# A two-layer decode step: keys and values as the streamed operand of TensorE, in column groups of four kv heads, and late loading of the first feed-forward weights

## The chip, the cores and the metric

The kernel runs on one core of one Trainium2 chip. The metric is the device time of one execution in microseconds (us). Times are medians of a few executions, with lowest and highest in brackets. A ratio is the one on record for the fast runs of two kernels in the same rounds on the same chip; it is not quite the quotient of the medians quoted beside it (they differ by up to 0.6%). Its 95% interval follows in square brackets. The kernel before was run again beside every experiment: its medians lay between 367 and 372 us from chip to chip, so kernels of different rounds are compared by their ratios. A run is called slow when it is more than 1.5% above the fastest run of the same kernel, and fast otherwise. Medians and ranges are of all runs: two of the five of v_stat were slow, and one each of early_w, before_6buf, best_4k (the profiled one) and best_half_4k. Stage times come from one profiled execution per kernel.

## The reference, cut to what matters

One token for each of four batch rows, 32 query heads, 8 kv heads, 4096 cached positions, head width 128, all bf16. The same attention and the same feed-forward are applied twice, with the same weights and caches, so each row needs its keys and its values twice. The kernels keep the transposed keys (K^T) of a row in memory between the layers and read K once; V is read twice.

```python
def _A_ref(x, k_cache, v_cache, wq, wo):
    q = ...                                       # x @ wq, 32 heads of 128
    k = jnp.repeat(k_cache, rep, axis=1)          # rep = 4 query heads a kv head
    v = jnp.repeat(v_cache, rep, axis=1)
    scores = jnp.einsum("bhqd,bhkd->bhqk", q, k) * (Dh ** -0.5)
    p = _softmax(scores, axis=-1)
    o = jnp.einsum("bhqk,bhkd->bhqd", p, v)
    return ... @ wo

x = x + _A_ref(_layernorm(x), A_k_cache, A_v_cache, A_wq, A_wo)
x = x + _B_ref(_layernorm(x), B_w_gate, B_w_up, B_w_down)
x = x + _A_ref(...)        # layer 2: the same caches and weights
x = x + _B_ref(...)
```

## The kernel before

The kernel works row by row: layer 1 of row b+1 shares a stretch of time with layer 2 of row b. In that stretch ("K/V stretch" below) a row's K arrives in chunks of 512 KB, DVE turns each into K^T, layer-2 scores of row b use the old K^T and layer-1 scores of row b+1 the new one, and V chunks of row b+1 follow. Then comes the "feed-forward stretch": output projection, feed-forward and query projection of row b+1, with the layer-2 V chunks of row b filling the gaps. DMA is issued in program order, into one ring of buffers.

In both attention products the cache is the *stationary* operand: a 128x128 block is loaded into the array and a few columns stream past it, 16 query columns for the scores, 4 probability columns for the values.

```python
KV_BUFS = 7                    # ring of 512 KB chunks of K and V
GH = 2                         # kv heads of one softmax round

def load_kv(cache, b, kvh, t, name):
    tl = kvin.tile([P, CH, Dh], BF16, name=name, tag="kv")
    src = cache[b, kvh].rearrange("(p c) d -> p c d", p=P)      # 4 KB a partition
    dq.dma_start(out=tl[:], in_=src[:, t * CH:(t + 1) * CH])
    return tl

def scores_head(sc, s, kt, kvh, qb):
    ...
    for g in range(G8):
        for be in range(BE):                  # 32 matmuls a head
            nc.tensor.matmul(sc[:, s, g, :], lhsT=kt[:, g, be // 2, :, be % 2],
                             rhs=qb[:, kvh, be].rearrange("p a h -> p (a h)"),
                             start=(be == 0), stop=(be == BE - 1))

def soft_exp(sc, gmax):
    ...                                       # DVE subtracts the maximum
    nc.scalar.activation(out=raw..., in_=sc..., func=ACT.Exp, scale=scale)   # contiguous

class Values: ...
    v = load_kv(A_v_cache, self.b, kvh, t, "v_t")
    for i in range(CH):                       # 16 matmuls a chunk
        c = t * CH + i
        nc.tensor.matmul(o, lhsT=v[:, i, :], rhs=pe[:, s, c, :],
                         start=(c == 0), stop=(c == C - 1))

def rest_weights(i): ...       # wq, wo, w_gate, w_up, w_down, one piece after each
                               # softmax round of the first attention
```

## Time and profile before

Median 372.08 us (371.13 to 372.81, 3 runs); the profiled span is 373.3 us. Stages are cut at the first score matmul of each row's K/V stretch and at the last layer-1 V chunk of that stretch, both read from the timeline.

| stage | us | sum |
|---|---|---|
| start, to the first scores of the first K/V stretch | 99.0 | 99.0 |
| three K/V stretches | 54.9, 49.7, 52.5 | 157.1 |
| three feed-forward stretches | 22.2, 27.6, 24.3 | 74.1 |
| tail: last layer-2 attention and feed-forward | 43.2 | 43.2 |

The page of the kernel before: first the busy time of the engines (us, share of the span, instructions), then GB/s in 40 slices, the chain of waits, and three groups (busy us, mean ns of one | idle before, what ended it).

```profile
PE 204.4 (55%) x6848; PEld 193.2 (52%) x6848; DVE 160.4 (43%) x502; ACT 26.5 (7%) x70; POOL 25.1 (7%) x70
...
GB/s 237 421 417 383 416 375 417 395 407 228 11 253 302 234 376 363 382 313 359 288 244 386 347 329 377 358 341 275 271 332 308 265 382 413 345 311 147 248 119 2
...
PE 38%; DMA 29%; issue 16%; DVE 15%; POOL 1%; ACT 1%; SPq 0%; ACTq 0%; POOLq 0%; DVEq 0%
...
L334 PE MATMUL ot<-pe,v_t 128*128 128x4 bf16 x2048 | 68.7, 167 | 77.2 <-DMA v_t<-in_A_v_cache_dram 60.1
...
L254 DVE STREAM_TRANSPOSE kt<-k_t 128x512 f32<-128x512 f32 x128 | 82.8, 686 | 26.9 <-DMA k_t<-in_A_k_cache_dram 16.8
...
L285 ACT ACTIVATE raw<-sc 128x256 bf16<-128x256 f32 x32 | 12.3, 383 | 222.6 <-DVE sc L281 222.6
```

No engine is full, and TensorE waits 60.1 us for V. DMA reaches 421 GB/s where nothing holds it up and falls to 11 GB/s at the first feed-forward (slice 11) and to 234 to 300 in the score phases. The kernel is a stream of cache bytes with holes in it.

What a chunk costs TensorE is seen in the timeline of the kernel before (start us, us, engine, line, operation, count):

```profile
270.64 1.85 PE L266 MATMUL sc<-qb,kt 128*128 128x16 bf16 x64
...
318.28 0.99 PE L334 MATMUL ot<-pe,v_t 128*128 128x4 bf16 x32
...
321.26 0.57 PE L334 MATMUL ot<-pe,v_t 128*128 128x4 bf16 x16
321.69 0.99 PE L166 MATMUL qps<-xn_bf,wq_sb 128*128 128x1 bf16 x32
...
370.00 0.59 PE L523 MATMUL xo_ps<-ident_bf,xoT 128*4 128x128 bf16 x4 [0.47 <-DVE xoT L520]
```

The 16 value matmuls of a chunk begin at 321.26 and the next group at 321.69: 0.43 us a chunk, about 27 ns for a weight load with its matmul. The Trainium skill ("TensorE: Matmul & The Clock Gate", Part 2, "Weight-path perf modes") says that weights of 128 bf16 columns take a fast load path; 27 ns for 128x128 cells agrees with it.

### The profile page before, as it was taken

To read this page: it belongs to the slowest core of one execution; us is meant where nothing else is said; L and a number is where in the kernel's file an instruction comes from. 1 tells how busy PE (TensorE), PEld (TensorE's weight loads), DVE (VectorE), ACT (ScalarE), POOL (GpSimd) and SP (SyncE) were. 2 spreads that over 40 slices of the span, in tenths; PEclk is the share of its full clock that TensorE was granted. 3 is DMA by queue.
4 is the path that set the end of the run, shared out by engine and by line. 5 is a ranking of instruction groups with operands and counts; after the bars stand their busy time and mean duration, and the time that the engine had idled before them with its cause. 6 is when DMAs were issued, how large, how long until landed. Compare 5 with 4: busy or idle time off the path is not lost.

```text
span 373.3 us, 14915 instructions
## 1 busy us (share of the span) xinstructions
PE 204.4 (55%) x6848; PEld 193.2 (52%) x6848; DVE 160.4 (43%) x502; ACT 26.5 (7%) x70; POOL 25.1 (7%) x70
## 2 busy tenths in 40 slices
PE   0435141337765545865555657656465557678645
PEld 0334141337665445764555647655465456677635
DVE  0854423303686553321777453127745523224104
ACT  0020000000011011000011010000101000001100
POOL 0000000000010111000111110000110100002000
DMA  7999999995078799999879899998888799984730
GB/s 237 421 417 383 416 375 417 395 407 228 11 253 302 234 376 363 382 313 359 288 244 386 347 329 377 358 341 275 271 332 308 265 382 413 345 311 147 248 119 2
DMA packets 36302, 115.52 MB, mean 309 GB/s; under 512 B 3208, under 2 KB 9104, under 8 KB 36240
## 3 DMA queue, kind: packets, MB, share of 16 engines
q1 hardware_dynamic: 36240, 114.58, 83.7%
q8 instruction: 53, 0.87, 0.9%
q14 instruction: 9, 0.07, 0.0%
HBM read 114.56 MB, written 0.00 MB: 307 GB/s over the span
## 4 chain that ended last, share of the span: by engine, by line
PE 38%; DMA 29%; issue 16%; DVE 15%; POOL 1%; ACT 1%; SPq 0%; ACTq 0%; POOLq 0%; DVEq 0%
DMA v_t<-in_A_v_cache_dram 29%; PE sc L266 11%; PE ot L334 10%; DVE kt L254 7%; PE qps L166 3%; PE y L190 3%; DVE colmax L273 2%; PE y L232 2%; PE hg L204 2%; PE hu L204 2%; PE x L293 1%; PE st L128 1%; DVE sc L281 1%; POOL gmax L275 1%; PE yf L190 1%
## 5 line engine op out<-in xcount | busy, mean ns | idle before, releaser
L334 PE MATMUL ot<-pe,v_t 128*128 128x4 bf16 x2048 | 68.7, 167 | 77.2 <-DMA v_t<-in_A_v_cache_dram 60.1
L334 PEld LDWEIGHTS <-v_t 128*128 128x128 bf16 x2048 | 63.7, 105 | 82.4 <-DMA v_t<-in_A_v_cache_dram 63.8
L254 DVE STREAM_TRANSPOSE kt<-k_t 128x512 f32<-128x512 f32 x128 | 82.8, 686 | 26.9 <-DMA k_t<-in_A_k_cache_dram 16.8
L266 PE MATMUL sc<-qb,kt 128*128 128x16 bf16 x2048 | 63.0, 175 | 17.5 <-issue 13.6
L266 PEld LDWEIGHTS <-kt 128*128 128x128 bf16 x2048 | 58.9, 104 | 20.0 <-issue 15.2
L273 DVE TENSOR_REDUCE colmax<-sc 128x8 f32<-128x256 f32 x32 | 13.4, 420 | 45.0 <-PE sc L266 45.0
L293 PE MATMUL x<-raw,ident_bf 128*32 128x64 bf16 x512 | 13.4, 238 | 31.1 <-ACT raw L285 28.6
L285 ACT ACTIVATE raw<-sc 128x256 bf16<-128x256 f32 x32 | 12.3, 383 | 222.6 <-DVE sc L281 222.6
L275 POOL PARTITION_ALL_REDUCE gmax<-colmax x32 | 11.9, 371 | 229.9 <-DVE colmax L273 149.7
L166 PE MATMUL qps<-xn_bf,wq_sb 128*128 128x1 bf16 (+1 forms) x640 | 20.2, 166 | 11.3 <-issue 10.1
L293 PEld LDWEIGHTS <-ident_bf 128*32 128x32 bf16 x512 | 9.8, 118 | 31.6 <-issue 30.9
L190 PEld LDWEIGHTS <-wo_sb 128*128 128x128 bf16 x640 | 19.8, 104 | 12.2 <-issue 12.2
L166 PEld LDWEIGHTS <-wq_sb 128*128 128x128 bf16 x640 | 18.9, 104 | 11.8 <-issue 11.2
L190 PE MATMUL y<-OT_bf,wo_sb 128*128 128x1 bf16 x512 | 15.8, 165 | 9.9 <-DVE OT_bf L338 6.7
L307 POOL PARTITION_ALL_REDUCE den<-cs x32 | 12.7, 398 | 85.7 <-DVE cs L304 85.7
L338 DVE TENSOR_TENSOR OT_bf<-ot,rden 128x8 bf16<-128x8 f32 (+1 forms) x23 | 3.5, 153 | 33.7 <-PE ot L334 33.7
L281 DVE TENSOR_TENSOR sc<-sc,gmax 128x256 f32<-128x256 f32 x32 | 13.5, 422 | 8.9 <-POOL gmax L275 8.7
L298 ACT CAST pe<-x 128x256 bf16<-128x256 f32 x32 | 11.9, 372 | 33.0 <-PE x L293 33.0
L304 DVE TENSOR_REDUCE cs<-raw 128x8 f32<-128x256 bf16 x32 | 12.4, 389 | 3.8 <-ACT raw L285 3.8
L171 DVE TENSOR_TENSOR q_bf<-qps,rstd 128x8 bf16<-128x8 f32 (+1 forms) x20 | 3.3, 170 | 24.0 <-PE qps L166 23.6
L197 DVE TENSOR_TENSOR XX<-XX,y 128x4 f32<-128x4 f32 (+1 forms) x9 | 1.4, 160 | 22.5 <-PE y L232 16.0
L179 DVE TENSOR_TENSOR qb<-qe,amask 128x128 bf16<-128x128 f32 (+1 forms) x23 | 7.8, 338 | 5.6 <-PE qe L177 5.5
(50 smaller groups left out, 113.2 us busy)
## 6 DMA issues: line engine op xcount, KB each, us to landing
v_t<-in_A_v_cache_dram SPq DMA_DIRECT2D x128, 512.0 KB, 7.4
k_t<-in_A_k_cache_dram SPq DMA_DIRECT2D x64, 512.0 KB, 8.8
wo_sb<-in_A_wo_dram SPq DMA_DIRECT2D x2, 2048.0 KB, 12.5
wq_sb<-in_A_wq_dram SPq DMA_DIRECT2D x2, 1024.0 KB, 9.2
wq_sb<-in_A_wq_dram SPq DMA_DIRECT2D x1, 2048.0 KB
wg_sb<-in_B_w_gate_dram SPq DMA_DIRECT2D x1, 1792.0 KB, 17.1
wu_sb<-in_B_w_up_dram SPq DMA_DIRECT2D x1, 1792.0 KB, 13.1
wd_sb<-in_B_w_down_dram SPq DMA_DIRECT2D x1, 1792.0 KB, 17.1
```

Source lines behind the costliest of these rows:

```text
L166: nc.tensor.matmul(qps[:, i, :], lhsT=wq_sb[:, k, m * Dh:(m + 1) * Dh], rhs=xn_bf[:, k, bs], start=(k == 0), stop=(k == KD - 1))
L190: nc.tensor.matmul(y[:, :, dk], lhsT=wo_sb[:, i, dk * P:(dk + 1) * P], rhs=rhs, start=(first and i == h0 and dk == 0), stop=(last and i == ...
L204: nc.tensor.matmul(h[:, m, :], lhsT=w_sb[:, k, m * P:(m + 1) * P], rhs=xn_bf[:, k, bs], start=(k == 0), stop=(k == KD - 1))
L254: nc.vector.transpose(out=self.kt[:, t * gt:(t + 1) * gt, bb].rearrange("p g c j -> p g (c j)"), in_=kf[:, :, bb])
L266: nc.tensor.matmul(sc[:, s, g, :], lhsT=kt[:, g, be // 2, :, be % 2], rhs=qb[:, kvh, be].rearrange("p a h -> p (a h)"), start=(be == 0), s ...
L273: nc.vector.tensor_reduce(out=colmax[:], in_=v, axis=AX.X, op=ALU.max)
L275: nc.gpsimd.partition_all_reduce(gmax.rearrange("p s h -> p (s h)"), colmax.rearrange("p s h -> p (s h)"), P, RED.max)
L281: nc.vector.tensor_tensor(out=w, in0=w, in1=gmax[:].unsqueeze(2).broadcast_to([P, GH, G8 * QD, rep]), op=ALU.subtract)
L293: nc.tensor.matmul(x[a * QS:(a + 1) * QS, :, :, cc, :], lhsT=ident_bf[:, cc * QS:(cc + 1) * QS], rhs=raw[:, :, :, a, :], start=True, stop= ...
L304: nc.vector.tensor_reduce(out=cs[:], in_=raw.rearrange("p s g a h -> p s h (g a)"), axis=AX.X, op=ALU.add)
L307: nc.gpsimd.partition_all_reduce(den.rearrange("p s h -> p (s h)"), cs.rearrange("p s h -> p (s h)"), P, RED.add)
L334: nc.tensor.matmul(o, lhsT=v[:, i, :], rhs=pe[:, s, c, :], start=(c == 0), stop=(c == C - 1))
```

## The change

The intent is to make the *cache* the streamed operand and the narrow queries and probabilities the stationary one, with the array split into four groups of 32 columns that work side by side. Four kv heads share one softmax round; a maximum over 512 columns and an exp with the maximum as bias replace DVE's subtraction and sum. The rest follows from it: V is read in rows of 2 KB (so that a chunk fits the new column order), exp writes its result permuted, the two halves of a value result are put together with masks (`sel_y`), and with the new tiles in memory only six of seven chunk buffers fit. Besides that, wo, w_gate, w_up and w_down are loaded behind the last V chunk of row 0 instead of during the first attention. The diff, cut to its core (renames, constants and the final recombination left out):

```diff
-GH = 2
-KV_BUFS = 7
+GH = 4
+KV_BUFS = 6
...
-def scores_head(sc, s, kt, kvh, qb):
-    for g in range(G8):
-        for be in range(BE):
-            nc.tensor.matmul(sc[:, s, g, :], lhsT=kt[...], rhs=qb[:, kvh, be]..., ...)
+def scores(kts, qb):                 # 32 matmuls for four heads
+    for s in range(2):
+        for be in range(BE):
+            for G in range(2):
+                for n in range(2):
+                    r0 = 32 * (2 * n + G)            # column group
+                    nc.tensor.matmul(sc[r0:r0 + 32, :],
+                        lhsT=qb[:, s, G * BE + be].rearrange("p a h -> p (a h)"),
+                        rhs=kt[:, be // 2, n * SN:(n + 1) * SN, be % 2],   # 512 columns
+                        ...)
...
+    nc.scalar.activation(out=p.rearrange("p g j c -> p g c j"),       # every 4th bf16
+                         in_=sc.rearrange("p (g c j) -> p g c j", g=HN, c=QD),
+                         func=ACT.Exp, bias=nm[:, 0:1], scale=scale, accum_out=ls[:])
...
+    src = A_v_cache[self.b, kvh].rearrange("(a q g) d -> q a g d", a=QD, g=KG)
-    for i in range(CH):
-        nc.tensor.matmul(o, lhsT=v[:, i, :], rhs=pe[:, s, c, :], ...)
+    for gl in range(HN):                 # 8 matmuls a chunk, on two column groups
+        for n in range(2):
+            r0 = 32 * (2 * n + G)
+            c0 = r0 + 16 * s + 8 * t
+            nc.tensor.matmul(self.acc[r0:r0 + 8, s], lhsT=pT[:, gl, c0:c0 + 8],
+                             rhs=v[:, :, n * HN + gl, :], ...)            # 256 columns
...
 # attend(), order of a row
+    sc2 = [scores(old K^T of four heads) for both groups]   # layer 2 of the row before
+    ... 8 K chunks turned, with the two softmax rounds between them ...
+    sc1 = scores([KT[i] for i in range(GH)], qb1[0])        # after all 8
...
+    if b1 == 0:      # after the last V of row 0
+        dq.dma_start(out=wo_sb..., ...); ... wg_sb, wu_sb, wd_sb
```

## The prediction

> **What bounds the kernel now.** Mostly the stream of keys, values and weights, broken by chains of compute. The page shows 114.58 MB loaded; in undisturbed stretches (the table of 10-us windows, 10 to 30 us) DMA moves about 418 GB/s, so the bytes alone need about 274 us of the 373.3. The rest is DMA idle or slow: nothing moves from 90 to 102 us (first feed-forward), 200 to 300 GB/s in the score phases of each batch row (100 to 130, 180 to 200, 250 to 270 us), about 10 us at the last feed-forward. No engine is full: PE 55%, DVE 43%. In the chain of waits the V load is only 29%, PE 38%, and "issue" 16%: pieces of 1.3 to 3.9 us in which PE waits for nothing but its instructions (the instruction queue moved 0.87 MB, as much as 2 x 6848 PE instructions of 64 B).
>
> **What the change removes.** 2048 score matmuls (a head, 32 of them plus loads, takes 0.86 us), 2048 value matmuls (0.43 us per 512 KB chunk) and 512 swap matmuls. It adds 512 matmuls of 512 columns, 1024 of 256 and 64 transposes; PE falls from 6848 to about 3900 matmuls. On DVE the score maximum, subtraction and sum (13.4 + 13.5 + 12.4 us) become 16 maxima of 512 columns and small operations, plus 32 accumulator reads: about 20 us less. POOL loses about 18 us. The 128 transposes of K (82.8 us busy, about 1.22 us a chunk in pairs) stay.
>
> **What decides it: do column groups run side by side?** This trace says yes: the 16 swap matmuls (four column groups, 64 columns) start within 0.17 us, and their cast follows 0.46 us after the first start. The Trainium skill ("TensorE: Matmul & The Clock Gate", Part 3) gives 2.38x for three column tiles at 512 columns, and 216 ns for one such matmul alone; 32 of them in four groups are then, as an estimate, 2.0 to 2.8 us for four heads, against 3.45 now. A value chunk alternates between two groups: about 0.45 us, as now. If they ran one after another, a score group would be 7 us and a chunk 0.85, and the kernel slower, about 400 us.
>
> **On the critical path.** (1) First feed-forward: its weights (10 MB, 24 us) now load behind the last V of row 0, under output projection, gate and up. The first scores of the next phase start near 90 us instead of 99. (2) A row's cycle is now 78.7, 75.7 and 77.1 us from its first score to the next row's (in the chain). I reckon about 68 to 72: fewer softmax rounds (2 groups, not 4), eight K chunks turned almost without interruption, scores 1.4 times as quick, fewer instruction stalls. DMA alone needs 60. (3) After the last K: 42.7 us now, about 37 then. Sum: 90 + 3 x 70 + 37 = 337.
>
> **What would show it.** Score matmuls of a quarter starting within tens of ns, a group of 32 in under 3 us; issue in the chain down to about 10%; DMA gap at the first feed-forward under 6 us; row cycle near 70 us; K transposes still 0.61 to 0.69 us each; mean rate about 340 GB/s.
>
> **What would make it wrong.** Column groups that serialize, through weight loads (the skill's "TensorEngine Tiling (Array Packing)", Restrictions, says column tiling disables fast weight load) or moving reads of every second bf16; V rows of 2 KB instead of 4 KB per descriptor slowing the stream; six buffers instead of seven running dry while softmax of four heads is awaited; instruction stalls that stay.
>
> Predicted 338 us, 318 to 364; faster 0.86, same 0.07, slower 0.07.

(In it, a row's cycle is quoted as 78.7, 75.7 and 77.1 us. Cut at the first score matmuls, as in the tables here, the three cycles of the kernel before are 77.1, 77.3 and 76.8. The 216 ns for a matmul of 512 columns stand in Part 2 of that page, not in Part 3, and hold at full clock.)

## The result, and the profile after

The kernel after takes 412.05 us (409.67 to 413.51, 4 runs) against 371.61 (369.93 to 372.81, 4 runs): ratio 1.1135 [1.1048, 1.1221]. It is slower by 11%, and outside the predicted range.

| stage | before | after | predicted |
|---|---|---|---|
| start | 99.0 | 102.7 | 90 |
| three K/V stretches | 157.1 | 168.7 | |
| three feed-forward stretches | 74.1 | 91.1 | |
| both, three rows | 231.2 | 259.8 | 3 x 70 = 210 |
| tail | 43.2 | 46.9 | 37 |
| profiled span | 373.3 | 409.4 | 337 |

Every stage is longer. The page of the kernel after, in the order in which before was shown, with the row of granted clock that before's page doesn't have:

```profile
PE 246.3 (60%) x3908; PEld 157.3 (38%) x3908; DVE 165.8 (40%) x513; ACT 34.0 (8%) x54; POOL 6.9 (2%) x22
...
PEclk9996565555656565655665656558555656556655
...
GB/s 273 312 348 384 367 268 334 378 375 277 82 294 210 382 270 336 367 347 183 270 237 338 355 239 366 322 307 170 276 215 387 241 333 362 331 193 61 359 95 2
...
L368 PE MATMUL acc<-v_t,pT 128*8 128x256 bf16 x1024 | 97.3, 397 | 42.2 <-DMA v_t<-in_A_v_cache_dram 39.4
L288 DVE STREAM_TRANSPOSE kt<-k_t 128x512 f32<-128x512 f32 x128 | 80.9, 683 | 35.8 <-DMA k_t<-in_A_k_cache_dram 35.8
...
L302 PE MATMUL sc<-kt,qb 128*32 128x512 bf16 x512 | 52.9, 590 | 16.5 <-DVE qb L210 16.5
L327 ACT ACTIVATE p<-sc,nm 128x512 bf16<-128x512 f32 x16 | 22.3, 1395 | 219.6 <-DVE junk L322 218.8
```

There are 43% fewer TensorE instructions, and TensorE is busy 42 us longer. The value products rose from 68.7 to 97.3 us. One exp takes 1395 ns for 512 columns, where before 256 took 383. The transposes of K are what they were. (The chain of waits of this profile could only be followed back over the last 38 us, so it isn't set beside the one of before.)

**The clock.** The row PEclk says that TensorE mostly ran near half clock. Its first three slices say 9, and before's page has no such row and says clock 1.000. Both are the absence of a record, not full speed. (In the windows of later sections, the 0.99 of best is so for the first 5 of its 12 us, and every 1.00 of best_half is so: their first records come at 99.6 and 322.3 us.) The timeline of the kernel after shows it; the first four lines are the first score group of the kernel (and the stationary loads that begin each four of its matmuls), the next two are the same four transposes of 128 columns at two times, then the same value chunk at two times:

```profile
25.73 3.60 PE L302 MATMUL sc<-kt,qb 128*32 128x512 bf16 x32 [0.52 <-DVE qb L210]
26.14 0.16 PEld L302 LDWEIGHTS <-qb 128*32 128x32 bf16 x4 [0.27 <-issue]
26.57 0.16 PEld L302 LDWEIGHTS <-qb 128*32 128x32 bf16 x4 [0.27 <-issue]
26.99 0.16 PEld L302 LDWEIGHTS <-qb 128*32 128x32 bf16 x4 [0.27 <-issue]
...
111.32 0.40 PE L335 MATMUL pt<-ident_bf,p 128*128 128x128 bf16 x4 [2.17 <-ACT p L327]
...
115.22 0.61 PE L335 MATMUL pt<-ident_bf,p 128*128 128x128 bf16 x4 [3.51 <-ACT p L327]
...
167.99 0.60 PE L368 MATMUL acc<-v_t,pT 128*8 128x256 bf16 x8
...
178.02 1.02 PE L368 MATMUL acc<-v_t,pT 128*8 128x256 bf16 x8
```

The windows around four of these, and the two stretches that follow the first score group, of the same kernel (window: length, busy us and count of PE, PEld, DVE, ACT, POOL, then granted clock, DMA share, GB/s):

```profile
111.30:111.75 0.45, 0.40 (x4) 0.23 (x4) 0.45 (x2) 0.00 (x0) 0.00 (x0) 1.00 0.69 255
115.20:115.85 0.65, 0.63 (x8) 0.61 (x8) 0.65 (x2) 0.00 (x0) 0.00 (x0) 0.50 0.75 265
...
178.00:179.05 1.05, 1.05 (x15) 0.45 (x13) 0.48 (x3) 0.00 (x0) 0.00 (x0) 0.50 1.04 402
25.70:29.40 3.70, 3.60 (x32) 1.08 (x32) 0.32 (x2) 0.00 (x0) 0.00 (x0) 1.00 1.03 420
29.90:33.20 3.30, 0.00 (x0) 0.00 (x0) 1.80 (x7) 1.48 (x2) 0.40 (x1) 1.00 1.03 395
33.40:57.10 23.70, 14.05 (x168) 6.97 (x168) 11.10 (x22) 1.59 (x3) 0.39 (x1) 0.50 0.96 351
```

Four transposes of 128 columns take 0.40 us where 1.00 was granted and 0.61 where 0.50 was. Four matmuls of 128 columns at the end of the kernel before took 0.59: half clock, under a heading of 1.000. The score group at 25.73 runs under "1.00" as well, and it starts four matmuls of 512 columns every 0.42 to 0.43 us. The Trainium skill ("TensorE: Matmul & The Clock Gate", Part 1) gives 426.7 ns as the distance of matmuls of 512 columns with the clock throttled to one half, its default, and 215.7 at full clock: this agrees with the first figure. The kernel after runs mostly at half clock (0.603 on its page, where the first 30 us without a record count as 1), the kernel before wherever its trace lets it be seen; and before the first record a profile shows 1. The first record of the kernel after is a grant of full clock at 29.85 us, half a microsecond after its first score group has ended, and 3.41 us later the clock is back at half: TensorE had nothing to do in between. Where two score groups follow each other, full clock comes in the middle of them, so their 64 matmuls take 6.48 us at 102.66 and not twice 3.60.

The prediction's own evidence agrees with half clock too: 16 swap matmuls of 64 columns on four column groups, started within 0.17 us, are four rounds about 53 ns apart, 0.83 ns a column.

This also answers what the prediction called decisive. Four transposes of 128 columns, 512 columns one after another, take 0.61 us with the latency of the last one; four matmuls of 512 columns on four column groups start every 0.43 us. The column groups do run side by side.

**The hole at the row's start.** The last part of the result is in the windows of 12 us from the first scores of the first K/V stretch, before and then after:

```profile
99.00:111.00 12.00, 7.35 (x259) 6.97 (x258) 9.80 (x22) 1.51 (x4) 1.53 (x4) 1.00 0.59 183
```

```profile
102.70:114.70 12.00, 6.84 (x70) 2.40 (x68) 8.73 (x21) 2.92 (x4) 0.77 (x2) 0.64 0.34 112
```

DMA moves 183 GB/s there in the kernel before and 112 in the kernel after. The timeline of the kernel after says why, in order of time:

```profile
102.66 6.48 PE L302 MATMUL sc<-kt,qb 128*32 128x512 bf16 x64
...
106.32 0.69 DVE L311 TENSOR_REDUCE m<-sc 128x1 f32<-128x512 f32 x1 [2.79 <-PE sc L302]
...
107.19 2.49 DVE L288 STREAM_TRANSPOSE kt<-k_t 128x512 f32<-128x512 f32 x4
...
108.52 5.44 SPq L284 DMA_DIRECT2D k_t<-in_A_k_cache_dram  x4
...
124.99 1.40 ACT L327 ACTIVATE p<-sc,nm 128x512 bf16<-128x512 f32 x1 [8.54 <-DVE junk L322]
```

Chunks of K lie ready in the ring, but their first transpose stands behind the row maximum in DVE's program, the maximum waits 2.79 us for the scores of a whole group of four heads, and only the transposes free chunk buffers. The next K loads are issued from 108.52 on. The last line is the exp of a later round; it matters below.

### The profile page after: what moved, and what is told of

It reads as the page before. It is cut to its first block, busy times and chain, and to the rows that moved or that the text cites. A ratio compares the mean times of both kernels' runs of the same rounds, so it can differ in the third digit from the quotient of the medians.

```text
span 409.4 us, 8903 instructions
## 1 busy us (share of the span) xinstructions
PE 246.3 (60%) x3908; PEld 157.3 (38%) x3908; DVE 165.8 (40%) x513; ACT 34.0 (8%) x54; POOL 6.9 (2%) x22
## 5 line engine op out<-in xcount | busy, mean ns | idle before, releaser
L368 PE MATMUL acc<-v_t,pT 128*8 128x256 bf16 x1024 | 97.3, 397 | 42.2 <-DMA v_t<-in_A_v_cache_dram 39.4
L368 PEld LDWEIGHTS <-pT 128*8 128x8 bf16 x1024 | 47.0, 111 | 74.8 <-issue 50.4
L302 PE MATMUL sc<-kt,qb 128*32 128x512 bf16 x512 | 52.9, 590 | 16.5 <-DVE qb L210 16.5
L327 ACT ACTIVATE p<-sc,nm 128x512 bf16<-128x512 f32 x16 | 22.3, 1395 | 219.6 <-DVE junk L322 218.8
L302 PEld LDWEIGHTS <-qb 128*32 128x32 bf16 x512 | 17.2, 134 | 44.7 <-issue 25.7
L311 DVE TENSOR_REDUCE m<-sc 128x1 f32<-128x512 f32 x16 | 11.0, 690 | 38.1 <-PE sc L302 38.1
L222 PE MATMUL y<-OT_bf,wo_sb 128*128 128x1 bf16 x512 | 14.9, 165 | 11.9 <-DMA wo_sb<-in_A_wo_dram 10.2
L388 PE MATMUL fin<-sel_o,o 128*128 128x8 f32 x64 | 15.4, 351 | 5.5 <-DVE o L376 5.5
L388 PEld LDWEIGHTS fin<-sel_o,o 128*128 128x128 f32 x64 | 14.2, 308 | 6.6 <-DVE o L376 6.6
L210 DVE TENSOR_TENSOR qb<-qe,sel 128x256 bf16<-128x256 f32 x32 | 11.8, 410 | 4.0 <-PE qe L205 4.0
L264 PE MATMUL y<-H_bf,wd_sb 128*128 128x1 bf16 (+1 forms) x280 | 8.6, 166 | 5.7 <-DMA wd_sb<-in_B_w_down_dram 3.7
```

The costliest lines, as they stand in the source:

```text
L210: nc.vector.tensor_tensor(out=qb[:, s], in0=qv[:, s].unsqueeze(2).broadcast_to([P, 2 * BE, 2 * QD, rep]), in1=sel2[:, s].unsqueeze(1).unsq ...
L222: nc.tensor.matmul(y[:, :, dk], lhsT=wo_sb[:, i, dk * P:(dk + 1) * P], rhs=rhs, start=(first and i == h0 and dk == 0), stop=(last and i == ...
L264: nc.tensor.matmul(y[:, :, dk], lhsT=wd_sb[:, k, dk * P:(dk + 1) * P], rhs=H_bf[:, k, :], start=(k == 0), stop=(k == KF - 1))
L302: nc.tensor.matmul(sc[r0:r0 + 32, :], lhsT=qb[:, s, G * BE + be].rearrange("p a h -> p (a h)"), rhs=kt[:, be // 2, n * SN:(n + 1) * SN, be ...
L311: nc.vector.tensor_reduce(out=m[:], in_=sc[:], axis=AX.X, op=ALU.max)
L327: nc.scalar.activation(out=p.rearrange("p g j c -> p g c j"), in_=sc.rearrange("p (g c j) -> p g c j", g=HN, c=QD), func=ACT.Exp, bias=nm[ ...
```

## The experiments

In these, "points" are per cent of the time of the kernel before in the same rounds; one point is 3.7 us. Of the seven runs of before beside v_stat7, half_sc7, exp_read and split7, three were slow.

| kernel | us (lowest to highest, runs) | ratio [95%] |
|---|---|---|
| after | 412.05 (409.67 to 413.51, 4) | 1.1135 [1.1048, 1.1221] |
| v_stat | 399.5 (393.72 to 400.39, 5) | 1.0813 [1.0725, 1.09] |
| v_four | 398.59 (398.24 to 400.98, 4) | 1.079 [1.0711, 1.0869] |
| v_wide | 411.88 (407.6 to 412.97, 4) | 1.1114 [1.1018, 1.121] |
| early_w | 421.89 (417.02 to 426.14, 4) | 1.1362 [1.1244, 1.148] |
| half_sc (wrong) | 378.85 (375.93 to 381.31, 4) | 1.0305 [1.021, 1.04] |
| exp_flat | 456.55 (455.39 to 461.25, 4) | 1.2446 [1.2331, 1.2561] |
| before_2k (wrong) | 362.76 (361.25 to 363.15, 4) | 0.9863 [0.979, 0.9936] |
| before_6buf | 389.4 (388.07 to 394.22, 4) | 1.0575 [1.0454, 1.0695] |
| v_stat7 | 389.45 (386.97 to 390.44, 4) | 1.0592 [1.0476, 1.0709] |
| half_sc7 (wrong) | 371.49 (369.4 to 372.52, 4) | 1.0106 [0.9997, 1.0215] |
| exp_read | 399.14 (397.01 to 400.54, 4) | 1.0865 [1.0711, 1.1019] |
| split7 | 371.01 (370.33 to 372.02, 4) | 1.0103 [1.0003, 1.0202] |
| best | 363.4 (362.73 to 363.92, 6) | 0.9793 [0.9739, 0.9847] |
| best_half (wrong) | 359.49 (357.12 to 360.11, 4) | 0.9674 [0.961, 0.9739] |
| best_half_4k (wrong) | 355.34 (353.39 to 358.89, 4) | 0.9623 [0.9539, 0.9708] |
| best_4k (wrong) | 362.73 (359.05 to 364.65, 4) | 0.9808 [0.9721, 0.9895] |
| best_four | 368.96 (367.75 to 371.22, 6) | 1.0014 [0.9963, 1.0065] |

The first theory (C in the texts below) was the clock: streamed columns cost twice what was reckoned. The rival (S) was the stream: DMA and DVE stand still at the start of a row because of order and buffers. Both turned out to hold parts, and neither the whole. The totals of v_stat, half_sc, v_stat7 and best_half_4k fell between the ranges that were expected, those of early_w, exp_flat, before_2k and before_6buf outside all of them, and that of exp_read 1 us under its range.

### Values stationary again (v_stat)

Only the value products go back to the form of before; scores, softmax, order and loads stay.

```diff
-                        nc.tensor.matmul(self.acc[r0:r0 + 8, s], lhsT=pT[:, gl, c0:c0 + 8],
-                                         rhs=v[:, :, n * HN + gl, :], ...)
+                            nc.tensor.matmul(self.acc[:, hl, :], lhsT=v[:, y, n * HN + gl, :],
+                                             rhs=pT[:, gl, c0:c0 + rep], ...)
```

> The changed kernel with one part undone: V is again the stationary operand (16 matmuls of 4 columns a chunk), all else as changed. Theory C (TensorE runs at half clock nearly everywhere, a streamed column costs 0.83 ns, so a value chunk costs 1.02 us instead of 0.43 us and the feed-forward stretches become TensorE-bound): chunk back to about 0.43 us, each of the three feed-forward stretches with values falls from about 30 us to 22 to 24 us, total 378 to 390 us. Theory S (the loss is the softmax chain of four heads, in which the six buffers run dry): total stays above 404 us, feed-forward stretches shorter but DMA idles as much after.

Measured: 399.5 us, 3.2 points less than after. The three feed-forward stretches fell from 91.1 to 81.3 us and the three K/V stretches stayed at 168.3. A feed-forward stretch in windows, after and then v_stat:

```profile
158.00:188.00 30.00, 27.79 (x522) 20.94 (x526) 10.65 (x51) 0.21 (x1) 0.00 (x0) 0.56 0.99 342
```

```profile
158.30:186.00 27.70, 19.67 (x642) 19.33 (x641) 7.58 (x45) 0.21 (x1) 0.00 (x0) 0.50 0.95 341
```

In the kernel after TensorE is busy 27.8 of 30 us there: it is the limit of that stretch. With stationary values it is busy 19.7. Of the 14.2 us between the two profiled spans, 9.8 come off the feed-forward stretches, 1.5 off the start and 2.5 off the tail; in the K/V stretch values were not the limit. The time came out between what the two theories expected, so neither covers it.

### Values on all four column groups (v_four) and on wider groups (v_wide)

In the change each value matmul takes 8 probability columns and half of the rows it makes are thrown away, on two of four groups. v_four splits each into two of 128 columns, one a group, with nothing thrown away. v_wide makes each matmul 32 columns wide, to see whether a busier array raises the clock; its extra rows are wrong.

```diff
 # v_four
+                        for y in range(HALF):
+                            r0 = 32 * (2 * n + y)
+                            nc.tensor.matmul(self.acc[r0:r0 + rep, hl, :],
+                                             lhsT=pT[:, gl, c0:c0 + rep],
+                                             rhs=v[:, y, n * HN + gl, :], ...)    # 128 columns
 # v_wide
-                        nc.tensor.matmul(self.acc[r0:r0 + 8, s], lhsT=pT[:, gl, c0:c0 + 8],
+                        nc.tensor.matmul(self.acc[r0:r0 + 32, s], lhsT=pT[:, gl, r0:r0 + 32],
```

> Values still stream, but as 16 matmuls of 128 columns on four column groups instead of 8 of 256 on two (no wasted rows), result gathered in bf16. Theory C: only the streamed columns per group and the clock count, so a chunk takes 4 x 107 = 0.43 us plus latency, and the total is that of the stationary form within 1.5%. If instead column groups or 4-column weight loads cost something of their own, a chunk stays at 0.6 us or more. Theory S: above 404 us.

> Wrong result on purpose: the values' stationary operand is 32 columns wide instead of 8, all else as changed. It streams the same columns but works four times as many cells. If the throttle grants clock by work done in the array and not by time busy, the granted clock rises clearly above 0.62 (0.75 or more), chunks fall towards 0.55 us and the total to 385 to 400 us. If it counts only busy time, clock 0.60 to 0.63 and 408 to 416 us.

Measured: v_four 398.59 us, the same as v_stat, so half of the streamed columns were waste and taking them away gains as much as the old form does. v_wide 411.88 us, the same as after, at a granted clock of 0.615 against 0.603: four times the cells at work does not raise the clock. (v_wide still passed the comparison with the reference although rows were wrong. The reference says why: run on a CPU with V set to zero, its output changes by 0.02 rms, beside an output of 2.5 rms. So the comparison can hardly see the attention, and a pass doesn't prove that a kernel is right.)

### Weights early again (early_w)

```diff
+    def rest_weights(i):     # wo, wo, w_gate, w_up, w_down, one a step of the first attention
...
-            dq.dma_start(out=wo_sb[:, :Hq // 2], ...)      # after the last V of row 0
```

> The changed kernel with the output and feed-forward weights loaded during the first attention again, between its values and keys. Theory W (the late weights cost time): first scores of the second phase at or before 99 us instead of 102.7, total 402 to 408 us. Theory C and S: late loading hides most of the load, so the total is the same or up to 5 us longer, 410 to 418 us.

Measured: 421.89 us, 2.3 points slower than after, and the first scores of the first K/V stretch at 109.86 us instead of 102.66. Late loading is a gain of about 7 us, as predicted in kind. It was hidden by the rest. The work still waits for the loads, though: in the output projection and feed-forward of row 0 of the kernel after TensorE waits 10.2 us for wo and 8.2 us for the other three.

### Half the score matmuls (half_sc, half_sc7)

No run here sets the clock. But half of the matmuls at half clock take what all would take at full clock. half_sc is v_stat with half of the score contraction left out.

```diff
-            for be in range(BE):
+            for be in (0, 2):
```

> Wrong result on purpose: the kernel with stationary values (v_stat) and only half of the score matmuls, 16 instead of 32 a group, so that scores take about 1.8 us at half clock, as the prediction had it for full clock. With v_stat's value chunks of 0.43 us this is the changed kernel as if TensorE ran at full clock. Theory C (the clock alone explains the miss): total 350 us or less. Theory S (K and V stretches are bound by the chain of softmax steps and the six buffers): 2 to 12 us under v_stat, 384 to 396 us.

Measured: 378.85 us, 5.1 points less than v_stat. A group is now 16 matmuls in 1.90 us, in a profile without any record of the clock (heading 1.000), the same pace as 32 in 3.60. A score group at half clock is 3.60 us against the 2.0 to 2.8 of the prediction, and as the rows stood this cost about 19 us. half_sc7 is the same on v_stat7 (below):

> Wrong result on purpose: v_stat7 with half of the score matmuls, that is the changed kernel with values and scores at the cost the prediction gave them, and seven buffers. If the clock (values and scores) and the buffers are the whole miss, the total comes near the predicted 338: 340 to 355 us. If there is a third cause of 15 us or more, 356 to 372 us.

Measured: 371.49 us, 4.9 points less than v_stat7. The clock of the scores, the value form and a seventh buffer together only bring the kernel to the time of before; something else was left.

### One buffer less, alone (before_6buf), and one more (v_stat7)

The kernel before with six buffers is one edited line. v_stat7 makes room for a seventh in v_stat by dropping a few small tiles; the query spread is then 16 narrow matmuls instead of 4.

```diff
 # before_6buf, from before
-KV_BUFS = 7
+KV_BUFS = 6
 # v_stat7, from v_stat
-KV_BUFS = 6
+KV_BUFS = 7
-    p1p = ctx.enter_context(tc.tile_pool(name="p1p", bufs=2))
+    p1p = ctx.enter_context(tc.tile_pool(name="p1p", bufs=1))
```

> The kernel before with six key and value buffers instead of seven, as in the change. Theory S says that the buffers run dry in the softmax chains, so one less costs 4 to 10 us: 374 to 380 us. If look-ahead does not matter: within 1%, 366 to 373 us.

> v_stat (values stationary again) with seven key and value buffers as before the change. Room for the seventh is made by one probability buffer less, smaller selection constants (q is spread by 16 narrow matmuls instead of 4) and no result buffer. Theory S as it now stands after before_6buf (a buffer less cost 22 us in the kernel before): 375 to 386 us, against 399 for v_stat. If look-ahead only matters in the order of the kernel before: 395 to 402 us.

Measured: before_6buf 389.4 us, 5.8 points slower than before by one buffer. v_stat7 389.45 us, 2.2 points faster than v_stat. The waits of TensorE for V (us in total, times, longest), of before and then of before_6buf:

```profile
PE ot L334 <- DMA v_t<-in_A_v_cache_dram: 60.1, 35, 8.9
```

```profile
PE ot L334 <- DMA v_t<-in_A_v_cache_dram: 83.8, 38, 8.9
```

TensorE waits 23.7 us longer for V, about all of the loss. (v_stat7 also carries the small edits that made room, so its 2.2 points are not those of the buffer alone.) The ring of chunks is what carries the stream over the holes, and the change gave up a seventh of it. Seven buffers in the changed kernel with its own value form (two column groups), or eight in the kernel before, were not run.

### Short rows of V alone (before_2k)

```diff
+            src = cache[b, kvh].rearrange("(a q g) d -> q a g d", a=4, g=8)
+            dq.dma_start(out=tl.rearrange("p (a g) d -> p a g d", g=8), in_=src[:, 2 * t:2 * t + 2])
```

> Wrong result on purpose: the kernel before with V loaded in rows of 2 KB per partition and descriptor, as the change loads it, instead of 4 KB. Theory D (the shorter V rows slow the stream): 376 to 384 us, and V stretches at 390 GB/s instead of 410. All other theories: within 1% of before, 366 to 374 us.

Measured: 362.76 us, 1.4 points *faster* than before (the order of the rows is wrong). Rows of 2 KB are not what cost the change its time. Why they gain here was not followed, and against the 2% margin the record calls this unclear.

### The exp (exp_flat, exp_read)

The exp of the change reads its scores in order and writes every fourth bf16. There are two ways to write contiguously: let the score matmuls put the columns in the wanted order (exp_flat), or let the exp read PSUM out of order (exp_read).

```diff
 # exp_flat: the streamed operand is read with steps of 128 bytes
-                            rhs=kt[:, be // 2, n * SN:(n + 1) * SN, be % 2],
+                            rhs=kt[:, be // 2, n * SN:(n + 1) * SN, be % 2].rearrange(
+                                "p (g c j) -> p g j c", g=HN, c=QD),
-        nc.scalar.activation(out=p.rearrange("p g j c -> p g c j"),
-                             in_=sc.rearrange("p (g c j) -> p g c j", g=HN, c=QD),
+        nc.scalar.activation(out=p.rearrange("p g j c -> p (g j c)"), in_=sc[:],
 # exp_read: the exp reads PSUM with steps of 128 bytes
-        nc.scalar.activation(out=p.rearrange("p g j c -> p g c j"),
-                             in_=sc.rearrange("p (g c j) -> p g c j", g=HN, c=QD),
+        nc.scalar.activation(out=p[:],
+                             in_=sc.rearrange("p (g c j) -> p g j c", g=HN, c=QD),
```

> The changed kernel with one order undone: the score matmuls read the keys in the order in which the probabilities are wanted, so that the exponential writes contiguous memory instead of every fourth bf16. Theory S (the chain of each softmax holds the buffers): exponential falls from 1.40 us to 0.6 to 0.8 us, total 398 to 408 us. Theory C: the chain is hidden, total within 2 us of 411. If the scattered moving read costs TensorE time, score groups take longer than 3.6 us, and this shows beside it.

> The changed kernel, but the exponential reads its scores from PSUM in the permuted order and writes contiguously, where the change reads in order and writes every fourth bf16. If the scattered write is what makes it 1.40 us, it falls to about 0.8 us, as in exp_flat, and the total to 400 to 408 us (16 softmax chains, about half of them on the critical path). If any permuted side costs as much: 1.3 to 1.5 us and 408 to 414 us.

Measured: exp_flat 456.55 us, a miss: the exp is short, but a score group doubles. Its timeline and its group:

```profile
131.75 7.26 PE L302 MATMUL sc<-kt,qb 128*32 128x512 bf16 x32 [3.65 <-DVE qb L210]
```

```profile
L328 ACT ACTIVATE p<-sc,nm 128x512 bf16<-128x512 f32 x16 | 11.0, 688 | 267.9 <-DVE junk L323 267.1 <-PE pt L335 0.7
```

exp_read 399.14 us, 2.7 points less than after. Its group:

```profile
L327 ACT ACTIVATE p<-sc,nm 128x512 bf16<-128x512 f32 x16 | 11.0, 687 | 217.7 <-DVE junk L322 217.1 <-PE pt L335 0.5
```

The exp fell from 1395 to 687 ns: the scattered write cost it 0.71 us, the scattered PSUM read nothing. ACT is 8% busy, but in 15 of the 16 softmax rounds the transposes of the probabilities wait for this exp (45.0 us in all in the kernel after, on its page, with the steps ahead of the exp), and the values wait for them.

### The order within a row (split7)

split7 is v_stat7 with the waits of the row's start taken apart. Scores of four heads are computed in two halves, each as soon as its two heads are turned; queries are spread earlier; two K chunks are turned before the first row maximum.

```diff
             sc2 = [scores([old[g * GH + i] for i in range(GH)], qb2[g]) for g in range(NG)]
-            gm2 = row_max(sc2[0])
             turner.step(2)
+            gm2 = row_max(sc2[0])
+            turner.step()
...
+            qb1 = {0: q_spread(q1_bf[:, :HG, b1])}
             turner.step()
             e2 = soft_exp(sc2[1], gm2)
+            sc1 = new_scores()
+            score_half(sc1, 0, KT, qb1[0])
...
-        sc1 = scores([KT[i] for i in range(GH)], qb1[0])
+        score_half(sc1, 1, KT, qb1[0])
```

> v_stat7 with the order changed: the first half of a score group (two heads) runs as soon as its two heads are turned, the spread of q goes before it, and two K chunks are turned before the first row maximum of a row. Theory S: each of the 7 chains that wait for K gets about 1.8 us shorter and DMA starts about 2 us earlier in each row, 8 to 16 us under v_stat7: 362 to 376 us. If the waits just move to the next step, within 4 us of v_stat7.

Measured: 371.01 us, 4.9 points less than v_stat7, the largest step of all, with the same work on every engine. The waits of the row maximum for scores (us in total, times, longest), of v_stat7 and then of split7:

```profile
DVE m L308 <- PE sc L299: 38.4, 13, 3.4
```

```profile
DVE m L315 <- PE sc L307: 14.8, 10, 2.5
```

DVE waits 23.6 us less, and the stream of K with it.

### All together (best), and what is still missing (best_half, best_4k, best_half_4k)

best is split7 with the exp of exp_read. best_half is best with half of the score matmuls, as above. The two with 4k read V in rows of 4 KB (`"(q a g) d -> q a g d"`), in a wrong order.

> split7 with the permuted read in the exponential (exp_read): stationary values, seven buffers, scores by half groups, short exponential. If the gains add (exp_read saved 12 us alone, split7 stands at 371): 357 to 364 us, 1.5 to 3.5% faster than the kernel before. If they overlap because both shorten the same wait: 365 to 370 us.

> Wrong result on purpose: best with half of the score matmuls, so that all terms stand at the cost that the prediction gave them. If the named causes (clock, buffer, exponential, order) are the whole miss: 338 to 350 us. If something unnamed is left: above 352 us.

> Wrong result on purpose: best with V in rows of 4 KB. If the stream counts here too: 352 to 359 us. If TensorE and the softmax chains bound it: 360 to 365 us, as best.

> Wrong result on purpose: best_half with V in rows of 4 KB, so the probabilities meet the wrong rows, at the same work. If the 2 KB rows hold the saturated value stretches at 385 GB/s: these rise to 405 to 420, and the total falls by 5 to 12 us to 348 to 354. If the row size does not matter: 356 to 362 us.

Measured: best 363.4 us, ratio 0.9793 [0.9739, 0.9847]. It is faster than both kernels; whether by more or less than 2% of before is not settled by that interval. In its 12 us from the first scores of the first K/V stretch, where the kernel after moved 112 GB/s, best moves 186:

```profile
94.60:106.60 12.00, 8.23 (x120) 3.26 (x120) 10.74 (x27) 2.14 (x5) 0.78 (x2) 0.99 0.58 186
```

best_half is 1.2 points under best, with intervals that touch. In v_stat the same halving was worth 5.1 points: once the order hides them, slow scores cost little. best_4k is the same as best. best_half_4k is 4 us under best_half with overlapping intervals. In windows of 1 us with DMA saturated (a DMA share of 1.02 or more, 15 to 300 us) the median rate was 387 GB/s in best and best_half, with V in rows of 2 KB, and 406 to 414 in before, best_4k and best_half_4k, with 4 KB (before_2k, 2 KB: 404). But best_4k gained nothing by it.

| stage | before | after | v_stat | best | best_half | predicted |
|---|---|---|---|---|---|---|
| start | 99.0 | 102.7 | 101.2 | 94.6 | 95.0 | 90 |
| three K/V stretches | 157.1 | 168.7 | 168.3 | 140.8 | 136.4 | |
| three feed-forward stretches | 74.1 | 91.1 | 81.3 | 83.2 | 87.9 | |
| both, three rows | 231.2 | 259.8 | 249.6 | 224.0 | 224.3 | 210 |
| tail | 43.2 | 46.9 | 44.4 | 42.5 | 37.9 | 37 |
| profiled span | 373.3 | 409.4 | 395.2 | 361.1 | 357.1 | 337 |

best_half is 20 us above the 337 of the prediction's sum: 5 in the start, 14 in the three rows, 1 in the tail. Its K/V stretches are 7 us a row shorter than before's, its feed-forward stretches 5 us longer. Where the stream of the first row loses time is seen in windows of 3 us of best_half:

```profile
95.00:98.00 3.00, 3.00 (x48) 1.11 (x37) 2.74 (x6) 0.00 (x0) 0.00 (x0) 1.00 0.01 4
98.00:101.00 3.00, 0.55 (x8) 0.00 (x0) 2.96 (x8) 0.25 (x1) 0.39 (x1) 1.00 0.77 251
...
137.00:140.00 3.00, 1.48 (x43) 1.32 (x41) 0.00 (x0) 0.00 (x0) 0.00 (x0) 1.00 1.05 383
...
161.00:164.00 3.00, 0.40 (x15) 0.32 (x13) 0.00 (x0) 0.00 (x0) 0.00 (x0) 1.00 0.90 303
```

In the middle DMA is saturated. At the row's start it stands still for 3 us and then moves some 250 GB/s until about 110. And at 161 to 164, in the feed-forward stretch, TensorE is busy 0.40 of 3 us while DMA falls to 303. The timeline of TensorE there (time idle in brackets; "issue" means that it waits for nothing that the profile shows):

```profile
147.01 1.36 PE L233 MATMUL hg<-xn_bf,wg_sb 128*128 128x1 bf16 x46 [1.42 <-issue]
...
153.48 0.73 PE L372 MATMUL acc<-pT,v_t 128*128 128x4 bf16 x22 [2.92 <-issue]
...
163.79 0.64 PE L191 MATMUL qps<-xn_bf,wq_sb 128*128 128x1 bf16 x18 [2.60 <-issue]
...
169.97 0.21 PE L202 MATMUL qe<-q_bf,sel 128*32 128x16 bf16 x5 [2.46 <-issue]
```

That is 9.4 us in one row. In the same stretch of the kernel before the chain of waits has "issue" for 0.70, 3.46, 3.85 and 1.24 us, 9.3 in all. The prediction expected fewer such stalls, and in the kernel after they did become few. The largest entries of TensorE's waits ended by "issue" (us in total, times, longest), of before and then of after:

```profile
PE sc L266 <- issue: 13.6, 6, 3.2
```

```profile
PE y L264 <- issue: 1.6, 2, 1.1
```

All such entries together are 43.4 us in before and 1.8 in after. With stationary values, and so 2048 value matmuls instead of 1024, they are back: 16.6 us in v_stat, 21.8 in best, 28.3 in best_half. So best_half doesn't have every term at the predicted cost: this one it lost again. In the trace, six transfers of 16 KB on the instruction queue start between 140 and 172 us, and one of them lies in or just before each of the four gaps above (144.64, 150.87, 161.42 and 167.49 us), which agrees with TensorE waiting for its instructions but doesn't show it. How much of the 14 us these stalls are, beside the hole at the row's start, was not tested.

### The change's own value form in the best kernel (best_four)

> best with the values streaming again, in the form of v_four (16 matmuls of 128 columns on four column groups, result gathered in bf16). If only the streamed columns per group count: 360 to 367 us, as best (363). If streaming has a cost of its own that the six-buffer runs hid: above 368 us.

best with values in the form of v_four, the best streamed form found: 368.96 us against 363.4 for the stationary form, 2.2 points slower, and no faster than before (ratio 1.0014 [0.9963, 1.0065]).

## Why the prediction was wrong

What held:

- Column groups run side by side. Four matmuls of 512 columns start every 0.43 us.
- Late weights are a gain: early_w is 2.3 points slower, with the first scores 7 us later.
- The K transposes stayed at 0.68 us each, and TensorE instructions fell to 3908. POOL lost 18.2 us.
- "fewer instruction stalls": TensorE's waits ended by "issue" fell from 43.4 to 1.8 us. (Whether issue fell to "about 10%" of the chain can't be said, as the chain of the kernel after could not be followed.)
- The named risk of six buffers was real (below). The named risks of serialized groups and of streamed reads of every second bf16 were not. The risk of 2 KB rows showed in the saturated rate (387 GB/s in best against 406 in best_4k), but no loss of time was shown by it.

The steps that failed:

1. **"about 0.45 us, as now" for a value chunk, and "2.0 to 2.8 us for four heads".** Both took columns at full clock. The heading "clock 1.000" was the absence of a record, not a measurement. The four transposes of 128 columns in 0.59 us at the end of before's own trace gave the half clock away. Measured: 1.02 us a chunk and 3.60 us a group, against 0.43 and four times 0.86 in the old form. So the value form lost where the prediction had a draw (v_stat, 3.2 points), and the scores gained nothing in TensorE time (half_sc: 5.1 points from full clock to half, as the rows stood).
2. **Six buffers as a mere risk, with no cost in the sum.** One buffer is 5.8 points in the kernel before (before_6buf) and, with the edits that made room for it, 2.2 in the changed one (v_stat7).
3. **"fewer softmax rounds (2 groups, not 4), eight K chunks turned almost without interruption".** A round of four heads is also a longer wait: DVE stood behind whole groups of scores (2.9 us on average, 3.4 at most, in 13 waits), and chunk buffers behind DVE. "DMA gap at the first feed-forward under 6 us" did not come either: the gap moved to the first scores, where the next K load was issued 5.9 us after they began, and DMA moved 112 GB/s over 12 us. Taking the order apart was worth 4.9 points (split7).
4. **The exp was not costed at all.** Its scattered write made it 1.40 us instead of 0.69, sixteen times on the path to the values: 2.7 points (exp_read).
5. **Weights "under output projection, gate and up", and first scores "near 90 us".** They came at 102.7 us, 12.7 later than predicted. TensorE waited 18.4 us for the late weights in the output projection and feed-forward of row 0: the loads were not under the work, the work waited for them. With the four repairs of best the first scores come at 94.6, while TensorE still waits 17.2 us for these weights.
6. **DVE "about 20 us less".** It was busy 165.8 us against 160.4. What this cost in time was not shown by an experiment.

The steps after, v_stat, v_stat7, split7, best take off 3.2, 2.2, 4.9 and 3.1 points: 111.35 to 97.93% of before. These are named and tested. The gap from best_half to the prediction, 20 us in the profiled spans, is placed (14 in the rows, 5 in the start), but how it divides between the hole at each row's start and the "issue" stalls that came back with the stationary values stays open.

## What to carry to other kernels

Before an operand is moved from the stationary side of TensorE to the streamed one, find the clock that this kernel's own matmuls run at, by timing some with many columns: at half clock a 128x128 load with 4 streamed columns took only 27 ns here, and 512 streamed columns took 427. When softmax rounds or score groups are made larger, follow what each frees and when, since a stream that lives on a few large buffers can lose as much by one buffer (5.8 points here) or by late releases (4.9) as by slow score matmuls (5.1). Write down the cost of every instruction whose access pattern changes, also on an engine that is 8% busy.

## What the Trainium skill lacked or had wrong

- "TensorE: Matmul & The Clock Gate", Part 1, says that the clock is released after about 3.4 us of sustained activity. The score groups agree: the first, of 3.60 us, was followed by a grant of full clock 4.1 us after its start. The feed-forward stretch of the kernel after does not: TensorE was busy 27.8 of 30 us and the mean granted clock was 0.56. Four times as many working cells a matmul (v_wide) left the mean at 0.615. What activity counts is not said.
- No page says that a profile shows clock 1.000 when there is no record of the clock. The score group at 25.73 us ran at half clock (0.43 us for four matmuls of 512 columns) under 1.00.
- "TensorE: Matmul & The Clock Gate", Part 3, measures 2.38x for three column groups and has no figure for four. Here four groups of 512 columns started every 0.43 us, a quarter of the half-clock time of their 2048 columns (0.83 ns each).
- "TensorEngine Tiling (Array Packing)", "When to Use Tiling", recommends to swap stationary and streamed operands with column tiling when the streamed side has at most 64 columns, in four column groups at 32. With 4 columns it lost here, mostly at half clock: a chunk took 1.02 us swapped and 0.43 unswapped, and the best swapped form cost 2.2 points (best_four against best). It lacks what the unswapped form takes: about 27 ns for each weight load with its matmul.
- "SBUF — State Buffer", "Door 1", says that access stays free while a 16-byte line is hit at least twice, up to strides of 8 bf16. For the streamed operand this agrees: steps of 4 bytes cost nothing, steps of 128 bytes took a score group from 3.60 to 7.26 us. For ScalarE writing every fourth bf16 it doesn't: 1395 ns against 687. Reading PSUM with steps of 128 bytes cost ScalarE nothing (687 against 688 ns).
- "DMA: Bandwidth & Descriptors", "Specifications", gives 512 bytes as enough for line rate. Saturated windows moved 387 GB/s with V rows of 2 KB in best and 406 to 414 with 4 KB, though 404 with 2 KB in before_2k.
